# Attention and MoE on one core: an order dropped from ACT's late work, and the power-of-two products moved to the transposes' banks

## The chip, the cores and the metric

The kernel runs on one core of one Trainium2 chip. The metric is the device time of one execution in microseconds. TensorE is called PE here, VectorE DVE, ScalarE ACT, GpSimd POOL, and SP is the queue that issues most transfers.

## The reference

Four batches, eight heads, 576 positions, head size 64. The attention has a bias that a small network computes from positions; its result goes through a gated MoE layer of width 512 and 1536.

```python
scores = scale * np.matmul(q, k.transpose(0, 1, 3, 2))
x = (psi_rel / psi_i)[..., None]
h = np.maximum(x @ w1 + b1, 0.0)
bias = h @ w2
scores = scores + bias.transpose(2, 0, 1)[None, :, :, :]
scores = scores - np.max(scores, axis=-1, keepdims=True)
attn = np.exp(scores)
attn = attn / (np.sum(attn, axis=-1, keepdims=True) + 1e-09)
attn_out = np.matmul(attn, v)
...
a = x @ w_a
b = x @ w_b
return (a * b @ w_out)
```

All inputs and outputs are float32.

## The kernel before, in words

**Tiles.** A unit is a batch, a pair of heads (A and B) and one of two chunks of rows (`UNITS`). Each unit has four tiles of 128 rows by 576 columns, in the second chunk a fifth for the left-over rows. `TILES` lists 144 tiles; the first 16 belong to the first four units (`u < NP`, `N0 = 16`), "opening" tiles here. They take their operands as float32; the later units split values into two 16-bit or rounded parts.

**One tile** goes through `attn_steps` in pieces. `qk_pair` (L450, for opening tiles two at a time) or `qk` (L428) makes the scores on PE. `soft1` (L465) adds the bias and takes the row minimum on DVE (L472), then the exponential on ACT (L477). One step later `soft2` (L500) forms the reciprocal of the row sum (L505 on POOL, L506 on DVE) and scales the row on POOL (L508). Two steps later `turn` (L514) transposes five blocks on PE (L521) into the tile `tp`. For an opening tile ACT copies it to SBUF in one piece (L526). For a later tile ACT casts it to float16 (L538), and DVE forms the rest: L539 for blocks 0 to 3 on all partitions, L540 for block 4, from partitions 64 to 127 only. Then `pv_first` (L480) or `pv` (L547) multiplies with the values into a PSUM tile of tag `pv` and splits the result into two float16 parts (ACT L495 and DVE L496; ACT L567 and DVE L569).

**PSUM.** A bank holds 2 KB per partition, which is 512 float32 numbers. `qk` takes two banks, `tp` (five blocks of 128 columns) takes two, of which the second holds block 4 alone, and `pv` takes one. All of these have one buffer, so `turn` and `pv` wait until the last reader of the former tile is done.

**Powers of two.** The values of a batch (`v_scale`, L189) and each group of four weight chunks (`wab_steps`, L297) are scaled by powers of two. ACT sums magnitudes along rows (L200, L266). `pow2_down` (L62) turns the column of sums into a row with a small product (L64) against the unit matrix, on one partition (values) or four (weights). DVE takes the maximum (L66), bounds it and keeps the exponent (L67, L68) and forms a diagonal (L72). `pow2_up` (L75) spreads the result over the 128 partitions with a second small product (L77), which DVE copies out (L79). Each of the two products, called `pr`, takes a tile of tag `pv` and so shares its one bank with the attention output. There are ten pairs in all. For the weights the second product, and with it the scaling (L283 on POOL, L286 on ACT, L287 on POOL), comes two steps of that generator after the first.

**Weights.** `w_load` (L235) issues the transfer of a chunk on SP, `w_unit` (L241) converts 64-bit bit patterns to float32 on ACT and DVE (L244 to L249).

**What sets the order.** On PE the order is that of the program text (`manual_schedule`). The generators for attention, weights and MoE are interleaved by `merge` in fixed proportions. On the other engines and on SP a planner orders instructions from their dependencies and its own estimate of when each is ready. `issue_after` adds an order between two instructions of one engine, without a wait for the end of the first. `late()` (L172) uses it: work traced inside goes behind the last score reduction on DVE (`ttrs`), the last exponential (`exps`) and the last opening copy on ACT (`evs`), and the last scaling on POOL (`pns`) traced so far. `evs` is filled only by opening tiles. Inside `late()` stand L200, the weight conversion and the parts of the weights, and the preparation of keys, queries and values of later units; the transfers follow `paced()`, behind the last bias transfer on SP.

**After the opening**, MoE blocks (`moe_block`, L635) are merged with the attention of the next batch: 24 products a chunk (L649) into one bank, the first 12 into its first half and the other 12 into its second half; ACT reads the first half (L657), DVE the second (L659).

Of the kernel before, what the change touches and what calls it, by code (L numbers as in the profile page):

```python
# [7 lines left out]
F32 = mybir.dt.float32  # L8
# [39 lines left out]
def attention_moe(ctx, tc, q0d, q1d, kd, vd, idn, wp, wa, wb, wo, lsw, lg, rl, out):  # L48
    nc = tc.nc
# [7 lines left out]
    g_d = dram.tile([FC, 128, TOK], F32, name="g_d")  # L57
    winv = cst.tile([128, FC, 2], F32, name="winv")
    xt, cpool, epool, xpool = [], [None], [None], [None]
    vsc = []  # L60

    def pow2_down(mx, n, tag):  # L62
        ps = pvp.tile([128, 512], F32, tag="pv", name="pr")
        nc.tensor.matmul(ps[0:n, 0:128], mx, tab["idn"], start=True, stop=True)  # L64
        m = att.tile([n, 1], F32, tag="p2m" + tag, name="p2m", bufs=2)
        nc.vector.reduce_max(out=m, in_=ps[0:n, 0:128], axis=AX.X)  # L66
        nc.vector.tensor_scalar(out=m, in0=m, scalar1=3.0e38, scalar2=2.0 ** -100, op0=ALU.min, op1=ALU.max)  # L67
        nc.vector.tensor_scalar(  # L68
            out=m.bitcast(I32), in0=m.bitcast(I32), scalar1=0x7F800000, scalar2=None, op0=ALU.bitwise_and
        )  # L70
        dg = att.tile([n, n], F32, tag="p2d" + tag, name="p2d", bufs=2)
        nc.vector.tensor_scalar(out=dg, in0=tab["idn"][0:n, 0:n], scalar1=m, scalar2=None, op0=ALU.mult)  # L72
        return dg

    def pow2_up(dg, n, tag):  # L75
        ps = pvp.tile([128, 512], F32, tag="pv", name="pr")
        nc.tensor.matmul(ps[:, 0:n], tab["one"][0:n, :], dg, start=True, stop=True)  # L77
        g = att.tile([128, n], F32, tag="p2g" + tag, name="p2g", bufs=2)
        nc.vector.tensor_copy(g, ps[:, 0:n])  # L79
        return g  # L80
# [85 lines left out]
        return tc.issue_after(rows_in[-1].ins) if rows_in else nullcontext()  # L166


    ttrs, exps, evs, pns = [], [], [], []

    @contextmanager
    def late():  # L172
        with ExitStack() as s:
            for x in (ttrs, exps, evs, pns):
                if x:
                    s.enter_context(tc.issue_after(x[-1].ins))
            yield
# [11 lines left out]
    def v_scale(b):  # L189
        mx = att.tile([128, NP], F32, tag="vmx", name="vmx", bufs=2)  # L190
        vfs = [load_v(b, hp) for hp in range(2)] if b else []
        yield
        for hp in range(NP):
            if b:
                junk = vf = vfs[hp]
            else:
                vf = st["vs", hp].rearrange("p x j d -> p (x j d)")
                junk = att.tile([128, 640], F32, tag="rv", name="junk", bufs=2)
            with late():
                nc.scalar.activation(junk, vf, AF.Abs, accum_out=mx[:, hp:hp + 1])  # L200
            junk = vf = None
            if b:
                vfs[hp] = None
                if hp + 2 < NP:
                    vfs.append(load_v(b, hp + 2))
            yield
        m1 = att.tile([128, 1], F32, tag="vm1", name="vm1", bufs=2)
        nc.vector.reduce_max(out=m1, in_=mx, axis=AX.X)
        dg = pow2_down(m1, 1, "v")
        yield  # L210
        if b:
            yield
        vsc.append(v_scales(pow2_up(dg, 1, "v"), b))
        yield
# [42 lines left out]
    def wab_conv(wt, raw):  # L257
        with late():
            return w_unit(wt, raw)

    def wab_size(f, j, wf, m):
        nm = "ab"[j]
        w16[nm, f] = w16t[:, f, j]
        c = 2 * (f % 2) + j
        with late():
            nc.scalar.activation(  # L266
                w16[nm, f][:, 0], wf.rearrange("p (k n) -> p k n", k=KC), AF.Abs, accum_out=m[:, c:c + 1]
            )
# [28 lines left out]
    def wab_steps(wt):  # L297
# [10 lines left out]
        for s in range(4 * np_ + 7):  # L308
            p, c = divmod(s - 7, 4)
            if 0 <= p < np_:  # L310
                if c == 0:
                    rms[p] = wab_scale(p, pow2_up(dgs.pop(p), 4, "w"))
                with late():
                    wab_parts(p, c, wfs.pop(s - 7), rms[p])
            p, c = divmod(s - 5, 4)
            if 0 <= p < np_ and c == 0:
                dgs[p] = pow2_down(ms.pop(p), 4, "w")
            if 1 <= s <= 4 * np_:
                p, c = divmod(s - 1, 4)
                if c == 0:  # L320
                    ms[p] = att.tile([128, 4], F32, tag="wm", name="wm", bufs=2)
                wab_size(2 * p + c // 2, c % 2, wfs[s - 1], ms[p])
            if s < 4 * np_:
                wfs[s] = wab_conv(*raws.pop(s))
                if s % 4 == 1 and s // 4 + 1 < np_:
                    fetch(s // 4 + 1)
            yield
# [14 lines left out]
    st = {}  # L342
# [171 lines left out]
    def turn(n, pool):  # L514
        u, t = TILES[n]
        c = UNITS[u][2]
        p = st.pop(("pn", n))
        tp = pool.tile([128, 5, 128], F32, tag="tp", name="tp", bufs=1)
        for x in range(5):
            c0 = min(128 * x, S - 128)  # L520
            nc.tensor.transpose(tp[:, x, :], p[:, c0:c0 + 128], tab["idn"])  # L521
        if u < NP:
            if t[0] == "A":
                st["pt", u] = epool[0].tile([128, 5, 256], F32, tag="pt", name="ptf", bufs=2)
            o = 128 * (t[0] == "B")
            evs.append(nc.scalar.copy(st["pt", u][:, :, o:o + 128], tp))  # L526
            return
        W = 512 + 128 * c
        if t in ("A0", "A2"):
            st["pt", u] = cpool[0].tile([128, 9, W], F16, tag="pt", name="pt", bufs=2)  # L530
        pt = st["pt", u]
        if t == "T":
            dst = pt.rearrange("p x (h w) -> p x h w", h=2)[:, :, :, 0:64]
            src = tp.rearrange("p x (h w) -> p x h w", h=2)
        else:
            o = {"A0": 0, "A1": 128, "B0": 256, "B1": 384, "A2": 64, "A3": 192, "B2": 384, "B3": 512}[t]
            dst, src = pt[:, :, o:o + 128], tp
        nc.scalar.copy(dst[:, 0:5], src)  # L538
        nc.vector.tensor_tensor(out=dst[:, 5:9], in0=src[:, 0:4], in1=dst[:, 0:4], op=ALU.subtract)  # L539
        nc.vector.tensor_tensor(  # L540
            out=dst[0:64, 4], in0=src[64:128, 4], in1=dst[64:128, 4], op=ALU.subtract
        )
# [33 lines left out]
    def attn_steps():  # L576
        vgen = [None]
        for n in range(NT + 3):
# [42 lines left out]
            if n >= 2 and n - 2 < NT:  # L621
                turn(n - 2, tpp)
# [120 lines left out]
    chunk_pool(0)  # L743
    qkp = ctx.enter_context(tc.tile_pool(name="qk0", bufs=1, space=PSUM))
    tpp = ctx.enter_context(tc.tile_pool(name="tp0", bufs=1, space=PSUM))
    pvp = ctx.enter_context(tc.tile_pool(name="pv0", bufs=1, space=PSUM))
    ctx.enter_context(tc.manual_schedule(engines={mybir.EngineType.PE}))
    wstack = ctx.enter_context(ExitStack())
# [140 lines left out]
```

## Time and profile before

| what | value |
|---|---|
| three runs, median (lowest to highest) | 876.42 us (870.93 to 877.58) |
| the profiled execution | 875.48 us |
| its span, first to last instruction | 873.4 us |
| mean granted clock of the PE | 0.945 |
| busy of the span | PE 780.3 us, DVE 546.0, ACT 512.5, POOL 308.4 |

The span is cut into stretches in the rows below. A line of the timeline is one instruction, or several in a row: start, duration, engine, line, operation, what it writes and reads, and in brackets how long the engine sat idle before it and what ended that. A line of the waits sums such idle times by who waited for whom. The granted clock is a share of 2.4 GHz; 0.50 is the lower of the two levels.

### The profile page before, as it was taken

To read this page: it belongs to the slowest core of one execution; us is meant where nothing else is said; L and a number is where in the kernel's file an instruction comes from. 1 tells how busy PE (TensorE), PEld (TensorE's weight loads), DVE (VectorE), ACT (ScalarE), POOL (GpSimd) and SP (SyncE) were. 2 spreads that over 40 slices of the span, in tenths; PEclk is the share of its full clock that TensorE was granted. 3 is DMA by queue.
4 is the path that set the end of the run, shared out by engine and by line. 5 is a ranking of instruction groups with operands and counts; after the bars stand their busy time and mean duration, and the time that the engine had idled before them with its cause. 6 is when DMAs were issued, how large, how long until landed. Compare 5 with 4: busy or idle time off the path is not lost.

```text
span 873.4 us, 16482 instructions
## 1 busy us (share of the span) xinstructions
PE 780.3 (89%) x5936; PEld 622.9 (71%) x5936; DVE 546.0 (63%) x1291; ACT 512.5 (59%) x1102; POOL 308.4 (35%) x480
## 2 busy tenths in 40 slices
PE   5865669878888698988999999999999999999998
PEld 1244446647777466765888888888898898888886
DVE  5545577879799667765587778777787665210100
ACT  4747557857686467764577667766776666331310
POOL 0022446747366412321244433432443344220210
PEclk9959688969998799999999999999999999999999
DMA  7897265724776345443444444444443432100001
GB/s 214 242 298 237 77 217 185 208 60 126 232 231 186 91 141 163 139 120 100 127 126 130 130 139 147 118 133 137 117 121 125 127 87 65 55 2 25 1 10 39
DMA packets 52596, 114.16 MB, mean 131 GB/s; under 512 B 5156, under 2 KB 9508, under 8 KB 52516
## 3 DMA queue, kind: packets, MB, share of 16 engines
q1 hardware_dynamic: 44336, 97.34, 36.9%
q10 hardware_dynamic: 8180, 15.77, 6.1%
q8 instruction: 47, 0.77, 0.4%
q14 instruction: 33, 0.27, 0.1%
HBM read 95.91 MB, written 17.18 MB: 129 GB/s over the span
## 4 chain that ended last, share of the span: by engine, by line
PE 66%; DVE 11%; DMA 10%; ACT 6%; issue 4%; SPq 1%; POOL 1%; ACTq 0%; DVEq 0%; POOLq 0%
PE ab L649 25%; PE o L698 17%; PE tp L521 8%; PE qk L444 8%; PE pv L555 5%; PE psta L136 3%; DMA rv<-vd 2%; DMA wraw<-wb 2%; DVE p L472 2%; DMA bias<-bias_d 2%; ACT p L477 1%; DVE ks L373 1%; DVE wt L246 1%; DVE wt L249 1%; DMA rvf<-vd 1%
## 5 line engine op out<-in xcount | busy, mean ns | idle before, releaser
L649 PEld LDWEIGHTS <-w16t 128*128 128x128 f16 x2592 | 254.1, 99 | 44.2 <-issue 12.7
L649 PE MATMUL ab<-x,w16t 128*128 128x256 f16 x2304 | 276.5, 277 | 0.0
L472 DVE CUSTOM_DVE_ANT_0 p<-qk,bias 128x576 f32<-128x576 f32 x144 | 108.7, 755 | 90.4 <-PE tp L521 80.1
L508 POOL TENSOR_SCALAR p<-p,rc 128x576 f32<-128x576 f32 x144 | 126.5, 879 | 70.9 <-DVE rc L506 64.2
L538 ACT CAST pt<-tp 128x640 f16<-128x640 f32 x128 | 88.3, 690 | 101.9 <-PE tp L521 101.4
L477 ACT ACTIVATE p<-p,mn 128x576 f32<-128x576 f32 x144 | 111.7, 776 | 47.6 <-DVE mn L472 45.3
L521 PE MATMUL tp<-idn,p 128*128 128x128 f32 x720 | 111.7, 289 | 20.3 <-DVE pt L540 8.1
L505 POOL TENSOR_SCALAR rr<-sm 128x1 f32<-128x1 f32 x144 | 31.2, 217 | 278.0 <-ACT p L477 274.8
L698 PE MATMUL o<-wos,gh 128*128 128x512 f32 x384 | 124.4, 405 | 0.0
L674 POOL TENSOR_TENSOR gl<-g,gh 128x256 fp32r<-128x256 f32 x96 | 72.6, 758 | 132.0 <-ACT gh L673 130.8
L521 PEld LDWEIGHTS tp<-idn,p 128*128 128x128 f32 x720 | 87.8, 148 | 39.0 <-issue 19.9
L539 DVE TENSOR_TENSOR pt<-tp,pt 128x512 f16<-128x512 f32 x128 | 88.0, 688 | 8.6 <-ACT pt L538 8.3
L659 DVE SCALAR_TENSOR_TENSOR g<-ab,wv,asb 128x256 f32<-128x256 f32 x84 | 40.3, 482 | 82.2 <-ACT asb L657 80.9
L698 PEld LDWEIGHTS o<-wos,gh 128*128 128x128 f32 x384 | 69.1, 190 | 17.8 <-issue 5.4
L444 PE MATMUL qk<-ks,qs 128*128 128x288 f32 x384 | 73.2, 313 | 4.9 <-DVE mn L472 3.8
L698 PE MATMUL o<-wos,gl 128*128 128x512 f32 x192 | 75.8, 395 | 0.0
L136 PE MATMUL psta<-h,w2s 128*32 128x288 f32 (+17 forms) x352 | 48.7, 558 | 25.4 <-ACT bo L154 12.2
L444 PEld LDWEIGHTS qk<-ks,qs 128*128 128x128 f32 x384 | 57.3, 192 | 10.5 <-DVE mn L472 5.3
L657 ACT ACTIVATE asb<-ab,wv 128x256 f32<-128x256 f32 x84 | 39.2, 468 | 40.4 <-PE ab L649 40.3
L673 ACT CAST gh<-g 128x256 fp32r<-128x256 f32 x96 | 38.7, 405 | 35.1 <-DVE g L659 34.8
L555 PE MATMUL pv<-pt,vs 128*64 128x320 f16 (+1 forms) x784 | 56.5, 298 | 0.0
L126 DVE TENSOR_SCALAR h<-u,lgs 128x576 f32<-128x576 f32 (+17 forms) x117 | 46.4, 456 | 14.9 <-PE psta L136 14.5
(92 smaller groups left out, 977.0 us busy)
## 6 DMA issues: line engine op xcount, KB each, us to landing
bias<-bias_d SPq DMA_DIRECT2D x128, 288.0 KB
rv<-vd SPq DMA_DIRECT2D x40, 320.0 KB
bias_d<-bo ACTq DMA_DIRECT2D x36, 295.5 KB
rk<-kd SPq DMA_DIRECT2D x24, 288.0 KB
wraw<-wa SPq DMA_DIRECT2D x12, 512.0 KB
wraw<-wb SPq DMA_DIRECT2D x12, 512.0 KB
wraw<-wo SPq DMA_DIRECT2D x12, 512.0 KB
rq<-q1d SPq DMA_DIRECT2D x16, 320.0 KB
```

What stands on the lines that cost most here:

```text
L136: nc.tensor.matmul(dst[32 * g:32 * g + 32], tab["w2"], hs[g][:, c0:c1], start=True, stop=True)
L444: nc.tensor.matmul(ps[:, hf, :HB], a, b[:, hf * HB:hf * HB + HB], start=(x == 0), stop=(x == len(prods) - 1))
L472: ttr = nc.vector.tensor_tensor_reduce(out=p.rearrange("p (a n) -> p a n", a=2), in0=ps[:, :, :HB], in1=bt.rearrange("p (a n) -> p a n", a=2),
L477: exps.append(nc.scalar.activation(p, p, AF.Exp, bias=mn, scale=-1.0, accum_out=sm))
L508: nc.gpsimd.tensor_scalar(out=p, in0=p, scalar1=rc, scalar2=1.0, op0=ALU.mult, op1=ALU.mult)
L521: nc.tensor.transpose(tp[:, x, :], p[:, c0:c0 + 128], tab["idn"])
L538: nc.scalar.copy(dst[:, 0:5], src)
L539: nc.vector.tensor_tensor(out=dst[:, 5:9], in0=src[:, 0:4], in1=dst[:, 0:4], op=ALU.subtract)
L555: nc.tensor.matmul(ps[64 * j:64 * j + 64, :N], vs[:, part, vb, j, :], pt[:, pb, j * N:j * N + N], start=(x == 0), stop=(x == len(TERMS) - 1),)
L649: nc.tensor.matmul(ab[:, j], w16[nm, f][:, pw, kk, :], xs[px][:, kk, :], start=(x % (3 * KC) == 0), stop=(x % (3 * KC) == 3 * KC - 1),)
L674: nc.gpsimd.tensor_tensor(out=gl, in0=g, in1=gh.bitcast(F32), op=ALU.subtract)
L698: nc.tensor.matmul(o, g[:, sl], wos[f][:, p], start=(f == 0 and x == 0), stop=(f == FC - 1 and x == 2))
```

## The change

The list `evs` goes, and with it the order of late ACT work behind the last opening copy. The `tp` tile is no longer allocated for each transpose: one tile of eight blocks of 128 columns (the same two banks) is allocated once, and the transposes write its blocks 0 to 4. A new function `pr_tile` hands out blocks 6 and 7 of it in turn, and both small products write there in place of a tile of tag `pv`.

```diff
--- before.py
+++ after.py
@@ -57,10 +57,17 @@
     g_d = dram.tile([FC, 128, TOK], F32, name="g_d")
     winv = cst.tile([128, FC, 2], F32, name="winv")
     xt, cpool, epool, xpool = [], [None], [None], [None]
-    vsc = []
+    vsc, tpt = [], []
+
+    prs = [0]
+
+    def pr_tile():
+        prs[0] ^= 1
+        return tpt[0][:, 6 + prs[0], :]
+
 
     def pow2_down(mx, n, tag):
-        ps = pvp.tile([128, 512], F32, tag="pv", name="pr")
+        ps = pr_tile()
         nc.tensor.matmul(ps[0:n, 0:128], mx, tab["idn"], start=True, stop=True)
         m = att.tile([n, 1], F32, tag="p2m" + tag, name="p2m", bufs=2)
         nc.vector.reduce_max(out=m, in_=ps[0:n, 0:128], axis=AX.X)
@@ -73,7 +80,7 @@
         return dg
 
     def pow2_up(dg, n, tag):
-        ps = pvp.tile([128, 512], F32, tag="pv", name="pr")
+        ps = pr_tile()
         nc.tensor.matmul(ps[:, 0:n], tab["one"][0:n, :], dg, start=True, stop=True)
         g = att.tile([128, n], F32, tag="p2g" + tag, name="p2g", bufs=2)
         nc.vector.tensor_copy(g, ps[:, 0:n])
@@ -166,12 +173,12 @@
         return tc.issue_after(rows_in[-1].ins) if rows_in else nullcontext()
 
 
-    ttrs, exps, evs, pns = [], [], [], []
+    ttrs, exps, pns = [], [], []
 
     @contextmanager
     def late():
         with ExitStack() as s:
-            for x in (ttrs, exps, evs, pns):
+            for x in (ttrs, exps, pns):
                 if x:
                     s.enter_context(tc.issue_after(x[-1].ins))
             yield
@@ -515,7 +522,7 @@
         u, t = TILES[n]
         c = UNITS[u][2]
         p = st.pop(("pn", n))
-        tp = pool.tile([128, 5, 128], F32, tag="tp", name="tp", bufs=1)
+        tp = tpt[0][:, 0:5, :]
         for x in range(5):
             c0 = min(128 * x, S - 128)
             nc.tensor.transpose(tp[:, x, :], p[:, c0:c0 + 128], tab["idn"])
@@ -523,7 +530,7 @@
             if t[0] == "A":
                 st["pt", u] = epool[0].tile([128, 5, 256], F32, tag="pt", name="ptf", bufs=2)
             o = 128 * (t[0] == "B")
-            evs.append(nc.scalar.copy(st["pt", u][:, :, o:o + 128], tp))
+            nc.scalar.copy(st["pt", u][:, :, o:o + 128], tp)
             return
         W = 512 + 128 * c
         if t in ("A0", "A2"):
@@ -743,6 +750,7 @@
     chunk_pool(0)
     qkp = ctx.enter_context(tc.tile_pool(name="qk0", bufs=1, space=PSUM))
     tpp = ctx.enter_context(tc.tile_pool(name="tp0", bufs=1, space=PSUM))
+    tpt.append(tpp.tile([128, 8, 128], F32, name="tp"))
     pvp = ctx.enter_context(tc.tile_pool(name="pv0", bufs=1, space=PSUM))
     ctx.enter_context(tc.manual_schedule(engines={mybir.EngineType.PE}))
     wstack = ctx.enter_context(ExitStack())
```

## Rows read from the trace of the kernel before

**Rows 1.** Stretches (us): busy PE, PEld, DVE, ACT, POOL; granted clock, DMA share, GB/s

```profile
46.00:125.00 79.00, 52.63 (x323) 36.29 (x323) 43.34 (x124) 46.95 (x108) 28.01 (x48) 0.73 0.62 203
125.00:180.00 55.00, 39.59 (x272) 28.82 (x272) 46.73 (x107) 40.99 (x93) 36.21 (x43) 0.88 0.65 193
180.00:300.00 120.00, 100.58 (x791) 80.77 (x790) 102.00 (x230) 79.15 (x163) 67.86 (x80) 0.90 0.53 161
400.00:757.00 357.00, 352.76 (x2865) 305.45 (x2863) 248.40 (x581) 224.64 (x479) 130.47 (x235) 1.00 0.39 116
```

**Rows 2.** Waits from 46 to 300 us: us in total, times, longest

```profile
ACT ptf L526 <- PE tp L521: 12.7, 8, 4.6
PE pr L77 <- DVE x L496: 9.1, 2, 5.6
PE tp L521 <- DVE pt L540: 8.1, 5, 3.0
PE pr L64 <- DVE x L496: 8.0, 3, 4.8
PE pr L64 <- DVE x L569: 5.9, 1, 5.9
ACT rv L200 <- DMA rv<-vd: 4.8, 3, 2.3
```

**Rows 3.** Chain that ended last, closing MoE stage: start us, us

```profile
804.84 31.45 PE ab L649 x288
```

**Rows 4.** Timeline of that stage, ACT: start us, us

```profile
807.52 0.47 ACT L657 ACTIVATE asb<-ab,wv 128x256 f32<-128x256 f32 x1 [2.05 <-PE ab L649]
810.14 0.47 ACT L657 ACTIVATE asb<-ab,wv 128x256 f32<-128x256 f32 x1 [1.12 <-PE ab L649]
```

**Rows 5.** Timeline from 84 to 89 us

```profile
84.89 0.16 DVE L208 TENSOR_REDUCE vm<-vmx 128x1 f32<-128x4 f32 x1 [0.72 <-ACT rv L200]
85.92 0.67 ACT L526 COPY ptf<-tp 128x640 f32<-128x640 f32 x1
88.48 0.58 PE L64 MATMUL pr<-idn,vm 128*1 128x128 f32 x2 [4.76 <-DVE x L496]
```

**Rows 6.** Timeline from 94 to 100 us

```profile
94.77 0.68 ACT L526 COPY ptf<-tp 128x640 f32<-128x640 f32 x1
98.61 0.58 PE L77 MATMUL pr<-p2d,one 1*128 1x1 f32 x2 [3.56 <-DVE x L496]
99.36 0.15 DVE L79 COPY p2g<-pr 128x1 f32<-128x1 f32 x1
```

**Rows 7.** Timeline from 126 to 131 us

```profile
126.42 0.29 DVE L540 TENSOR_TENSOR pt<-tp,pt 64x128 f16<-64x128 f32 x1
130.26 0.58 PE L77 MATMUL pr<-p2d,one 4*128 4x4 f32 x2 [5.57 <-DVE x L496]
```

**Rows 8.** Timeline from 175 to 182 us

```profile
175.33 0.29 DVE L540 TENSOR_TENSOR pt<-tp,pt 64x128 f16<-64x128 f32 x1
179.45 0.59 PE L64 MATMUL pr<-idn,wm 128*4 128x128 f32 x2 [5.89 <-DVE x L569]
181.06 0.27 DVE L66 TENSOR_REDUCE p2m<-pr 4x1 f32<-4x128 f32 x1
```

**Rows 9.** Timeline, two places where the bank is read late

```profile
155.30 0.38 PE L64 MATMUL pr<-idn,wm 128*4 128x128 f32 x2 [0.59 <-ACT w16t L266]
159.85 0.29 DVE L540 TENSOR_TENSOR pt<-tp,pt 64x128 f16<-64x128 f32 x1
162.17 0.76 DVE L472 CUSTOM_DVE_ANT_0 p<-qk,bias 128x576 f32<-128x576 f32 x1
...
199.09 0.38 PE L64 MATMUL pr<-idn,wm 128*4 128x128 f32 x2 [1.11 <-ACT w16t L266]
203.16 0.29 DVE L540 TENSOR_TENSOR pt<-tp,pt 64x128 f16<-64x128 f32 x1
205.26 0.75 DVE L472 CUSTOM_DVE_ANT_0 p<-qk,bias 128x576 f32<-128x576 f32 x1
```

## The prediction

> **What bounds the kernel now.** I read first the table of stretches. From 400 us to 757 us the PE is busy 352.76 of 357 us at the full clock of 2.4 GHz, and the change touches nothing there; what can move lies ahead of it [rows 1]. From 46 to 125 us the PE is busy 52.63 of 79 us at a granted clock of 0.73, with DVE and ACT a little over half busy: a stretch of latencies, in which engines wait for one another in turn. From 125 to 300 us DVE is busy 148.7 of 175 us and comes close to being the bound, while the PE still idles for some 35 us.
>
> Then the waits of this stretch, by who released them [rows 2]. Of the PE's idle time the largest shares stand before the tiny power-of-two products (name pr): 9.1 us in two waits and 8.0 us in three for the second half of the attention output (x, L496), which empties the one bank that pr shares with pv, and 5.9 us for the same step of the later tiles (L569). These 23.0 us are what the second part of the change aims at. 8.1 us are transposes that wait for the last reading of their bank (L540). ACT idles 12.7 us ahead of the eight opening copies (L526) that wait for the transposes.
>
> **What a product waits for in its new place.** Blocks 6 and 7 lie in the second 2 KB of the tile, with block 4, the fifth transpose. Does a write to an unread part of a bank wait for a reader of another part? In the closing MoE stage 288 products run without a gap from 804.84 us for 31.45 us [rows 3], 24 to a chunk, so 2.62 us a chunk. L657 reads only the first half of a chunk's bank, which is written after 1.31 us; it starts at 807.52 and 810.14 us, that is at 804.84 plus 2.62 and 5.24, when the second half is done too [rows 4]. So this program orders work by bank, and I take it that pr will wait until ACT's copy (L526, later L538) and DVE's L540 have read block 4.
>
> The Trainium skill says why (PSUM — Partial Sum Buffer, section "PSUM bank collisions raise a hardware error"): two engines may not be in the same bank on the same 32 partitions at once, at other columns either, so software orders by bank and quarter of the partitions, not by address. On the bank the trace agrees, 2.62 us a chunk and not 1.31; no row here shows the quarter. By the quarter the sum would be 868.0 us in place of 870.5 (third rival, worked out there).
>
> **The change, part by part.**
>
> (a) The products leave pv's bank: 20 uses of two PE passes each, unchanged in number and length. Four long stalls matter; the others are short or bound by their own operand.
> 1. The product at 88.48 us: its operand's reduction ended at 85.05 us, and the copy of block 4 ends at 85.92 + 0.67 = 86.59 us [rows 5]. Gain 1.9 us.
> 2. The product at 98.61 us: the copy ends at 95.45 us, so 3.1 us at most. But the product after it, in the same bank, needs L79, which stands on DVE at 99.36 us behind weight work [rows 6]. If that order stays the gain is 0. The order of DVE is planned anew, so I take half, 1.5 us.
> 3. The product at 130.26 us: L540 ends at 126.42 + 0.29 = 126.71 us [rows 7]; raw 3.5 us. DVE has little slack from here on, so I take 3.0.
> 4. The product at 179.45 us: L540 ended at 175.62 us, raw 3.8 us. The next product waits for L66 at 181.06 us, which is queued on DVE [rows 8]. Bounds 0 and 3.8, taken 1.9.
> Together 8.3 us, between 0 and 12.3.
>
> (b) The same products now wait where they did not before. After 125 us the reading of block 4 ends with L540, deep in a busy DVE queue. In seven places the trace has pr before the L540 of the tile transposed just ahead of it. The two worst: pr at 155.30 us, L540 ending at 160.14; pr at 199.09, L540 ending at 203.45 [rows 9]. The other five are 1.2 to 2.9 us each, and the seven add to 18.3 us of PE time. Behind the waiting product stand MoE products, the next scores, and through them the score reduction L472 on DVE. Only what arrives later than DVE would have taken it costs. At 155.30 some 2.9 us of PE work follow, so the scores would end at about 163.1 us where L472 started at 162.17: 0.9 us. At 199.09 some 4.2 us follow: 207.7 against 205.26, 2.5 us [rows 9]. In the other five DVE would come later anyway. Taken 3.4 us, bounds 0 and 18.3.
>
> (c) The transposes' tile is now allocated once. Blocks 0 to 3, in the first bank, may start after L539; only block 4 waits for L540, of 0.29 us. On the 8.1 us in five waits [rows 2] that is at most some 2 us; DVE is the later one there, so I take 0.7. The cost on this side is that block 4 must also wait for L66 or L79 to have read the product. In the trace these reads end before the fifth transpose of the next tile, or within a few tenths of it: nothing, so long as DVE keeps that order.
>
> (d) Late work on ACT (the sums of magnitudes L200 and L266, the weight conversion L244, the casts L286) need no longer follow the last opening copy. It still follows the last exponential, so it can rise only into the idle time ahead of a copy, and this is only while the first 16 tiles are turned; afterwards the removed order held nothing back. In about three of the eight idles [rows 2] an operation of 0.6 to 0.7 us that needs no new data directly follows the copy, and its rise would start the next exponential up to 1 us sooner. Against that: a fetched tile that is late in truth now holds up the copy behind it. L200 already waits 4.8 us in three waits for its transfer [rows 2], but there the copy stands behind it already. Bounds: 4 us lost, 3 won; taken 1.0 won. The transfers themselves are on SP; earlier reading frees their buffers sooner by the same 1 us at most.
>
> The sum: 8.3 + 0.7 + 1.0 - 3.4 = 6.6 us. Not all will reach the end: later stretches have their own limits (transfers, a busy DVE), so I let three quarters through, 5.0 us. Against the profiled execution of 875.48 us (span 873.4) that is 870.5 us. The median of the three times shown is 876.42, 0.94 us above the profiled one.
>
> **Rivals.**
> - The planner follows. DVE's and ACT's orders are made from the dependencies; with the new ones L66 and L79 rise and L540 is drawn ahead. Then (a) is had in full, 12.3 us, (b) costs nothing: 12.3 + 0.7 + 1.0 = 14.0, or 861.5 us. For it: in rows 6 and 8 the reductions stand behind work that was put there because the product was due late. Against: DVE has little room after 125 us.
> - The stall only moves. Places 2 and 4 gain nothing because the reading on DVE stays where it was; with 1.9 + 3.0 - 3.4 the time is 874.0 us.
> - Order by quarters of a bank. The first product of a pair writes one or four partitions, L540 reads partitions 64 to 127 (L540 in the code). If the order is kept for each 32 partitions, first products wait for ACT's copy alone. Both waits priced in (b) belong to first products (L64), so (b) falls to nothing, and three quarters of 10.0 us gives 868.0 us. Rows 4 can't tell, since both sides there use all partitions.
> - Slower: the bank that the products now share is read later than the one they left. Where DVE keeps L540 as late as in rows 9 and has no slack before the next L472, all seven waits pass through: 18.3 us against the 6.4 us of places 1 to 3, so 875.5 + 11.9 = 887.4 us. It decides from 139 us on. For it: DVE is busy 85% there. Against: in five of the seven places DVE would not have been ready.
>
> **How the numbers follow.** Chances: forecast 0.36, planner follows 0.20, stall moves 0.15, quarters 0.12, slower 0.17. About 1% (8.8 us) is what a measurement of this kernel can tell from no change. Below 867.7 us lie all of "planner follows", half of "quarters" and three tenths of the forecast: 0.37. Above 885.2 us lies most of the last: 0.16. The rest, 0.47, is within 1%. The range reaches from 858, where (a), (c) and (d) are had at their best (12.3 + 2 + 3), to 885 at the slower case's near edge; the forecast's own range is 866 to 876.
>
> **What would show it.** In the changed profile no pr may wait for L496 or L569 any more. If I am right, waits of pr for L526, L538 or L540 stand in their place, about half as long in total before 180 us; the PE's busy share from 46 to 180 us rises and with it the granted clock; L472 starts sooner after the stalls at 130 and 179 us. Wrong in (b) if pr never waits for L540, or if such waits add to 10 us or more with DVE idle behind them. Wrong in (d) if ACT's waits for transfers grow by more than 2 us with an opening copy queued behind them. From 400 us on nothing should differ but the start.

## The result and the profile after

| | before | after |
|---|---|---|
| median of 20 runs each, us | 875.96 (870.93 to 879.60) | 883.88 (876.51 to 889.59) |
| after / before, 95% interval | | 1.009 (1.0069 to 1.0112) |
| span of the profiled execution, us | 873.4 | 886.0 |
| mean granted clock | 0.945 | 0.927 |

The change makes the kernel 7.9 us slower by the medians. 870.5 us was forecast, a gain; the time lies inside the range (858 to 885), near its slow edge, on the wrong side of no change. The two profiled executions differ by 12.6 us, more than the medians, because after's is one of its longer ones, 4 us above the median. The readings below are of these two executions and account for those 12.6 us. After's line numbers are before's plus seven (L64 is L71, L540 is L547), and the product's tile is now named `tp`.

The table of stretches after, which answers to [rows 1] (same columns):

```profile
46.00:125.00 79.00, 55.03 (x305) 37.30 (x303) 44.09 (x124) 46.75 (x107) 27.19 (x48) 0.67 0.63 202
125.00:180.00 55.00, 44.16 (x292) 31.88 (x290) 42.36 (x98) 38.20 (x86) 30.21 (x38) 0.81 0.61 183
180.00:300.00 120.00, 99.22 (x749) 78.86 (x748) 100.52 (x218) 78.56 (x162) 65.65 (x77) 0.86 0.50 156
400.00:757.00 357.00, 350.30 (x2845) 302.00 (x2844) 252.57 (x588) 227.80 (x487) 132.69 (x238) 0.99 0.41 119
```

Read the counts and the clock, not the busy time. From 125 to 180 us the PE is busy for longer than before (44.16 against 39.59 us), with 20 instructions more, at a clock of 0.81 against 0.88: it works more slowly. So the prediction's sign, a busy share from 46 to 180 us that rises and the granted clock with it, came only in its first half, and a higher busy share alone is no gain. From 180 to 300 us 749 instructions run where 791 ran. From 400 us nothing is new: the work comes later and takes as long.

The waits after from 46 to 300 us, by who waited for whom, which answer to [rows 2] (total us, times, longest; rows that bear on the argument):

```profile
PE tp L71 <- ACT ptf L533: 6.0, 4, 2.9
PE tp L528 <- DVE pt L547: 5.9, 4, 3.0
ACT rv L207 <- DMA rv<-vd: 5.1, 4, 2.1
PE tp L71 <- ACT rv L207: 5.0, 1, 5.0
PE tp L84 <- DVE pt L547: 4.7, 2, 2.3
PE tp L71 <- DVE pt L547: 3.9, 2, 2.0
...
PE tp L84 <- ACT wt L251: 2.6, 1, 2.6
...
PE tp L528 <- DVE p2g L86: 2.5, 2, 1.3
...
PE tp L71 <- ACT x L574: 1.7, 1, 1.7
```

No product waits for the attention output any more: the 23.0 us behind L496 and L569 are gone. In their place stand 6.0 us behind the opening copy (L533) and 4.7 + 3.9 us behind the reading of block 4 (L547). Three more rows belong there, though the profile names ACT in them. L207 (5.0 us) sums magnitudes of values, but the product that waits there is one of the weights. The timeline shows the real releaser: L547 ends at 162.11 + 0.29 = 162.40 us, and the product starts 0.15 us later. So it is with the other two: L547 ends at 147.34 and 181.59 us, the products start at 147.49 and 181.74. In all, seven waits of 17.9 us stand behind L547, and with the 6.0 us the 23.0 us have come back whole under other names. One row is new in kind: transposes (L528) wait 2.5 us for the reading of a product (L86). The timeline at the place of 5.0 us, which is the first of [rows 9], and at the second:

```profile
162.11 0.29 DVE L547 TENSOR_TENSOR pt<-tp,pt 64x128 f16<-64x128 f32 x1
162.55 0.58 PE L71 MATMUL tp<-idn,wm 128*4 128x128 f32 x2 [5.00 <-ACT rv L207]
167.83 0.76 DVE L479 CUSTOM_DVE_ANT_0 p<-qk,bias 128x576 f32<-128x576 f32 x1 [1.09 <-PE tp L528]
...
207.16 0.29 DVE L547 TENSOR_TENSOR pt<-tp,pt 64x128 f16<-64x128 f32 x1
207.60 0.59 PE L71 MATMUL tp<-idn,wm 128*4 128x128 f32 x2 [1.91 <-DVE pt L547]
208.12 3.90 PE L656 MATMUL ab<-x,w16t 128*128 128x256 f16 x24
213.91 0.76 DVE L479 CUSTOM_DVE_ANT_0 p<-qk,bias 128x576 f32<-128x576 f32 x1 [2.12 <-PE tp L528]
```

Follow the second place. In [rows 9] the product ran at 199.09 us, ahead of L540; now it starts 0.15 us after that reading has ended. The 24 MoE products behind it take 3.90 us. Before, they took 2.79:

```profile
199.41 2.79 PE L649 MATMUL ab<-x,w16t 128*128 128x256 f16 x24
```

The difference is the clock: after, the granted clock is 0.50, the lower level, from 208 to 210 us; before, it is 1.00 from 199 to 203 us. DVE's next score reduction (L479) then has been idle for 2.12 us when its scores come: 213.91 us against 205.26.

The starts of the products tell where the time came from. "Shift" is after's start less before's, "step" its change from the line above (us). Fourteen of the twenty products are listed; one of the six left out matters below, the product at 165.08 us, which starts at 170.35 us after (shift +5.3).

```
before   after   shift  step   what released it after
 54.63   57.56   +2.9   +2.9   opening copy L533
 81.39   83.14   +1.8   -1.2   opening copy L533
 88.48   88.61   +0.1   -1.6   opening copy L533   (place 1)
 98.61   94.50   -4.1   -4.2   opening copy L533   (place 2)
 99.56   97.81   -1.8   +2.4   L86, reading of the product before
130.26  127.66   -2.6   -0.9   no wait             (place 3)
139.65  139.96   +0.3   +2.9   L547
146.14  147.49   +1.4   +1.0   L547
155.30  162.55   +7.3   +5.9   L547
179.45  181.74   +2.3   -5.0   L547                (place 4)
194.22  199.52   +5.3   +3.0   L547
199.09  207.60   +8.5   +3.2   L547
271.48  281.17   +9.7   +1.2
279.93  292.23  +12.3   +2.6   L547
end             +12.6
```

The opening products do gain: at 130 us after is 2.6 us ahead. Behind 130 us it loses 15.2 us, and of the seven places with L547 all but place 4 add to that.

What one such stretch costs the PE, between the same two products, before (first line) and after (second):

```profile
139.65:207.90 68.25, 54.84 (x385) 39.07 (x384) 58.68 (x139) 47.05 (x107) 40.29 (x48) 0.87 0.49 142
```

```profile
139.96:216.87 76.91, 59.94 (x385) 41.71 (x385) 58.23 (x137) 45.09 (x101) 37.45 (x46) 0.80 0.42 125
```

The stretch grows by 8.7 us. The same 385 PE instructions take 5.1 us more at the lower clock, and the PE idles 3.6 us more. DVE does almost the same work (58.2 against 58.7 us) and idles 18.7 us in place of 9.6: it waits more, too.

### The profile page after: what moved, and what is told of

It reads as the page before. It is cut to its first block, busy times and chain, and to the rows that moved or that the text cites. A ratio compares the mean times of both kernels' runs of the same rounds, so it can differ in the third digit from the quotient of the medians.

```text
span 886.0 us, 16591 instructions
## 1 busy us (share of the span) xinstructions
PE 792.2 (89%) x5936; PEld 628.8 (71%) x5936; DVE 548.5 (62%) x1291; ACT 513.5 (58%) x1102; POOL 306.0 (35%) x480
## 4 chain that ended last, share of the span: by engine, by line
PE 66%; DVE 10%; DMA 9%; ACT 8%; issue 5%; SPq 1%; POOL 0%; ACTq 0%; DVEq 0%
PE ab L656 24%; PE o L705 17%; PE qk L451 8%; PE tp L528 8%; PE pv L562 5%; DMA rv<-vd 3%; PE psta L143 3%; DVE p L479 2%; DMA bias<-bias_d 2%; ACT p L484 2%; DMA wraw<-wo 1%; DVE wt L253 1%; DMA rvf<-vd 1%; DVE wt L256 1%; DVE wt L252 1%
## 5 line engine op out<-in xcount | busy, mean ns | idle before, releaser
L479 DVE CUSTOM_DVE_ANT_0 p<-qk,bias 128x576 f32<-128x576 f32 x144 | 108.7, 755 | 97.1 <-PE tp L528 85.1
L528 PE MATMUL tp<-idn,p 128*128 128x128 f32 x720 | 112.0, 290 | 20.1 <-DVE pt L547 6.4
L528 PEld LDWEIGHTS tp<-idn,p 128*128 128x128 f32 x720 | 87.7, 147 | 39.5 <-issue 23.0
L546 DVE TENSOR_TENSOR pt<-tp,pt 128x512 f16<-128x512 f32 x128 | 88.0, 688 | 8.7 <-ACT pt L545 8.6
```

What stands on the lines that cost most here:

```text
L479: ttr = nc.vector.tensor_tensor_reduce(out=p.rearrange("p (a n) -> p a n", a=2), in0=ps[:, :, :HB], in1=bt.rearrange("p (a n) -> p a n", a=2),
```

## The experiments

The theory after this reading: late reading. The products moved after 125 us inherit the readers of the transposes' tile, chiefly L547. Rival one: the dropped order (`evs`) lets late ACT work delay the opening copies. Rival two: holding one tile for all transposes costs something by itself. All ratios are to the kernel before on the same chip.

**The order alone.** Before, with `evs` left out of `late()` only.

```diff
-            for x in (ttrs, exps, evs, pns):
+            for x in (ttrs, exps, pns):
```

> The kernel before with only the list of opening copies taken out of the late work's order; products and transposes' tile as before. Late reading (the loss comes from later products that wait in the shared bank for L540): nothing or a small gain, ratio 0.997 to 1.002. Dropped order (the loss comes from fetched work that stands in front of an opening copy): 6 to 9 us slower, ratio 1.007 to 1.010, and the delay is there by the 16th score reduction, at about 112 us.

Measured: 874.47 against 875.84 us, 0.9981 (0.9951 to 1.001).

**The products alone.** After, with `evs` put back in `late()`.

> The changed kernel with the order behind the opening copies put back, so that only the products' place and the one kept tile are new. Late reading: as slow as the changed kernel, ratio 1.007 to 1.011, the loss setting in after 139 us. Dropped order: no slower than before, ratio 0.995 to 1.000, since the four stalls before L496 and L569 are gone.

Measured: 883.01 against 875.84 us, 1.0078 (1.0051 to 1.0105). The two together: all of the loss comes with the products, and the order is worth nothing that can be measured.

**Which products.** The first two pairs of the values and of the weights (four in all, "opening" below) run up to 130 us, the other six ("later") after it. Here only the opening ones use the transposes' tile; `w` tells the four kinds of call apart (values or weights, first or second product).

```diff
-    def pr_tile():
+    def pr_tile(w):
+        i = prs[1][w] = prs[1].get(w, -1) + 1
         prs[0] ^= 1
-        return tpt[0][:, 6 + prs[0], :]
+        return tpt[0][:, 6 + prs[0], :] if i < 2 else pvp.tile([128, 512], F32, tag="pv", name="pr")
```

> The changed kernel with the order dropped, but of the ten pairs of products only the first two of the values and the first two of the weights (those of the opening tiles, up to about 131 us) go to the transposes' banks; the later six pairs stay in pv's bank. Late reading: the 2.6 us that the changed kernel was ahead at the 20th score reduction are kept or mostly kept, ratio 0.994 to 0.999, and no product waits for L540 (here L547 less a few lines). Dropped order: slower than before by 6 to 9 us, ratio 1.007 to 1.010.

Measured: 870.65 against 875.84 us, 0.9936 (0.9911 to 0.996). No product waits for L547 in its trace.

And the reverse, the later ones alone (`i >= 2`):

> The counterpart: the first two pairs of each kind stay in pv's bank, the later six go to the transposes' banks, the order is dropped. Late reading: slower by the whole loss after 139 us without the gain ahead of it, 9 to 14 us, ratio 1.010 to 1.016. Dropped order: slower by 6 to 9 us, with the delay there before 112 us.

Measured: 881.21 against 875.84 us, 1.0059 (1.0032 to 1.0087), less than expected. Its waits from 46 to 300 us (rows of products behind a bank's readers; others left out) show both banks at once:

```profile
PE pr L71 <- DVE x L503: 6.4, 2, 5.4
PE tp L84 <- DVE pt L547: 6.2, 4, 2.3
PE pr L84 <- DVE x L503: 5.3, 2, 3.0
PE tp L71 <- DVE pt L547: 4.9, 2, 3.0
PE tp L71 <- ACT wt L251: 4.9, 1, 4.9
PE tp L71 <- ACT vs L414: 2.9, 1, 2.9
```

The opening products wait for the attention output as before, the later ones for L547: eight waits, 18.9 us with the last two rows, whose products also start 0.15 us after an L547 has ended. So the change consists of a gain up to 130 us and a loss after it. The sizes don't add: 0.9936 and 1.0059 would make no change, and after is at 1.009, so the later products cost more beside moved opening ones (1.009 / 0.9936 = 1.0155) than alone.

**The tile by itself.** Before, with one tile allocated for all transposes and the products left in their old bank.

```diff
+    tpt.append(tpp.tile([128, 8, 128], F32, name="tp"))
...
-        tp = pool.tile([128, 5, 128], F32, tag="tp", name="tp", bufs=1)
+        tp = tpt[0][:, 0:5, :]
```

> The kernel before with only the transposes' tile allocated once for all; products stay in pv's bank, the order behind the opening copies stays. The planner gives the same order on every engine, so only the waits of the transposes change. If the part (c) was sized rightly: 0 to 2 us faster, ratio 0.998 to 1.000, and the 8.1 us of transposes that wait for L540 shrink by 1 to 2 us. A rival in which the kept tile itself costs (more waits on the transposes): slower, ratio above 1.003.

Measured: 875.63 against 875.43 us, 1.0001 (0.9982 to 1.002). Its waits, and the timeline at the end of one:

```profile
PE tp L521 <- DVE pt L540: 8.1, 5, 3.0
```

```profile
261.66 0.29 DVE L540 TENSOR_TENSOR pt<-tp,pt 64x128 f16<-64x128 f32 x1
...
262.10 0.45 PE L521 MATMUL tp<-idn,p 128*128 128x128 f32 x1 [2.98 <-DVE pt L540]
```

The transposes wait for L540 exactly as in [rows 2], 8.1 us in five. The first of them writes block 0, in the other bank from block 4, and starts only after block 4 is read (261.95 us). One tile in place of many costs nothing by itself, and it frees nothing.

**By bank or by tile.** After, with the two readings in `turn` exchanged: block 4 (now L546) ahead of blocks 0 to 3 (now L549).

```diff
-        nc.vector.tensor_tensor(out=dst[:, 5:9], in0=src[:, 0:4], in1=dst[:, 0:4], op=ALU.subtract)
...
+        nc.vector.tensor_tensor(out=dst[:, 5:9], in0=src[:, 0:4], in1=dst[:, 0:4], op=ALU.subtract)
```

> The changed kernel with the two readings of a later tile in the other order: block 4 first, then blocks 0 to 3, so that the bank which the products share comes free 0.7 us sooner and the first bank 0.3 us later. Late reading: some seven to ten waits of products shorter by up to 0.7 us each and what follows from them, 3 to 7 us off the changed kernel, ratio to before 1.001 to 1.006. If the loss has another cause (the order, the planner's new order as such): as slow as the changed kernel, 1.007 to 1.011.

Measured: 881.19 against 875.43 us, 1.0073 (1.0052 to 1.0095), which can't be told from after's 1.009. It lies in the range named for another cause, but the exchange did not free the products sooner, as it was meant to, so the time decides nothing. The timeline shows why:

```profile
156.41 0.29 DVE L546 TENSOR_TENSOR pt<-tp,pt 64x128 f16<-64x128 f32 x1
...
156.72 0.69 DVE L549 TENSOR_TENSOR pt<-tp,pt 128x512 f16<-128x512 f32 x1
...
157.56 0.59 PE L71 MATMUL tp<-idn,wm 128*4 128x128 f32 x2 [4.97 <-DVE pt L549]
```

Block 4 has been read by 156.70 us. The product, which writes block 6 or 7 beside it, starts 0.15 us after L549 has read the *other* bank (157.41 us). So do seven more products of this run. Here the program orders a write behind all readers of the tile, whatever bank they read.

**The order again**, now where the products gain: opening_moved with `evs` kept.

> The opening products alone moved, as in the run opening_moved, but with late work still behind the opening copies. If dropping the order is worth nothing: the same as opening_moved, ratio 0.991 to 0.997. If the order helps (products_moved was 10 us ahead at the 20th score reduction, the changed kernel 2.6): faster than opening_moved by 3 to 8 us, ratio 0.985 to 0.990.

Measured: 871.48 against 875.43 us, 0.9948 (0.9924 to 0.9972), beside 0.9936 without: no difference.

**Out of the way of L547.** The opening products stay in the transposes' tile; the later six go into the MoE products' three banks (tag `ab`).

```diff
-        return tpt[0][:, 6 + prs[0], :]
+        return tpt[0][:, 6 + prs[0], :] if i < 2 else mps.tile([128, 512], F32, tag="ab", name="pr", bufs=3)
```

> Opening products in the transposes' banks as in opening_moved; the later six pairs take a turn in the three buffers of the MoE products (tag ab), whose last readers are two chunks back. Late reading: no product waits for L540 or for L569 any more, 3 to 7 us faster than opening_moved, ratio 0.985 to 0.991. If a later wait takes the place (the next MoE chunk waits for the product's reading on DVE): the same as opening_moved, 0.991 to 0.997, with waits of L649 (here L656) for L66 or L79.

Measured: 866.12 against 875.43 us, 0.9883 (0.9864 to 0.9902). The two longest of the products' waits that are left:

```profile
PE tp L71 <- ACT ptf L533: 8.4, 4, 3.6
...
PE pr L84 <- DVE p2d L79: 6.0, 2, 3.8
```

The first row is opening products behind the copy. The second is a product that waits for its own operand.

**A bank of its own.** The opening products get a bank of a pool that is opened beside that of the bias network (`eq`), the later ones stay in `ab`.

```diff
-        return tpt[0][:, 6 + prs[0], :]
+        return opp[0].tile([128, 512], F32, tag="pr", name="pr", bufs=1) if i < 2 else mps.tile([128, 512], F32, tag="ab", name="pr", bufs=3)
```

> Opening products in a bank of their own (the one that is free until the MoE's three banks are allocated), later products in the MoE rotation as in later_in_ab; the order is dropped. If sharing the transposes' tile costs in the opening too (there 8.4 us of first products wait for the opening copies L533): 2 to 5 us faster than later_in_ab, ratio 0.982 to 0.986. If the opening has other limits (the operand of the product, the readings on DVE, transfers): the same as later_in_ab, 0.986 to 0.991.

Measured: 858.77 against 876.12 us, 0.9800 (0.9782 to 0.9818), faster than either expectation: sharing the transposes' tile costs in the opening too.

The same with `evs` kept:

> As own_bank, with late work kept behind the opening copies. If dropping the order is worth nothing, as opening_order_kept against opening_moved showed: within 0.4% of own_bank. If it helps where no product waits for an opening copy: 3 us or more slower than own_bank.

Measured: 857.55 against 876.12 us, 0.9789 (0.9767 to 0.981): 18.6 us below before, and better than both kernels; it can't be told from own_bank. Its longest waits of products, then the first stretch, here (first line) and in own_bank (second):

```profile
PE pr L71 <- ACT w16t L273: 8.5, 4, 4.0
...
PE pr L84 <- DVE p2d L79: 7.4, 2, 5.3
```

```profile
46.00:125.00 79.00, 54.63 (x373) 38.35 (x374) 51.43 (x146) 54.90 (x127) 39.35 (x57) 0.84 0.75 234
46.00:125.00 79.00, 57.88 (x345) 39.86 (x345) 49.80 (x137) 52.74 (x121) 34.61 (x55) 0.72 0.72 235
```

The products now wait mostly for their own operands (the sums of L273, the diagonal of L79). From 46 to 125 us the PE does 373 instructions where it did 323 in [rows 1], at a clock of 0.84 against 0.73. In own_bank it does 345, at 0.72: more work gets done in both, and the higher clock is not what both share.

**The later products alone in `ab`**, the opening ones in pv's bank as before.

> Opening products in pv's bank as before, only the later six pairs in the MoE rotation; the order is dropped. The share of the gain that comes after 139 us alone: if the waits for L569 and L496 there (5.9 and 5.6 us with the slow clock behind them) are what counts, 4 to 8 us faster than before, ratio 0.991 to 0.995; if most of later_in_ab's gain comes from the opening, 0.996 to 1.000.

Measured: 874.01 against 876.12 us, 0.9964 (0.9938 to 0.999), at the near edge of the range for "mostly the opening"; its interval takes in both ranges.

All ratios with the order dropped, by place:

| | later in `pv` | later in `tp` | later in `ab` |
|---|---|---|---|
| opening in `pv` | 0.9981 | 1.0059 | 0.9964 |
| opening in `tp` | 0.9936 | 1.0090 | 0.9883 |
| opening in own bank | | | 0.9800 |

## Why the prediction was wrong

**The step that failed is (b).** It named the wait, its reason and the two worst places, and then took 3.4 of the raw 18.3 us: "Only what arrives later than DVE would have taken it costs", and "In the other five DVE would come later anyway". Far more passed through. After, seven waits behind L547 add to 17.9 us; six are places that the prediction had listed, and the seventh is place 4, which it had not. At those six the shift grows by 2.9, 1.0, 5.9, 3.0, 3.2 and 2.6 us, 18.6 in all, of which 2.0 are given back at 170.35 us. At 155.30 us a cost of 0.9 us was forecast and L479 came 5.7 us late; at 199.09 us 2.5 were forecast and it came 8.7 us late in all, after a shift of 2.9 us at 190 us. The medians give 18 us as well where the opening products are in `tp`: the later ones in `tp` against `ab` are 1.009 / 0.9883 = 1.021. With the opening ones in `pv` the same step is 1.0059 / 0.9964 = 1.0095, only 8 us of 18.9 us of waits. So (b) was 8 to 18 us, not 3.4, and not always the whole wait.

The working held DVE's times fixed and asked when the PE would come. DVE's reading frees the tile, the product waits for it, the scores stand behind the product, and DVE waits for the scores: one loop, in which a delay on either side can delay both; in the stretch above PE and DVE both idle more. "DVE would come later anyway" was read from a trace without the new waits. Beside that, the work behind the stall ran at a lower clock, 5.1 of the 8.7 us of that stretch, for which the sum had no term.

The loop is not all of it. At the first place of [rows 9] the score reduction just ahead of the one at 167.83 us already came 4.6 us late, and DVE had not been idle before it. Its scores were done by 156.85 us, but the planner had put weight work (L252 to L256) ahead of it. Before, and then after:

```profile
155.52 0.74 DVE L472 CUSTOM_DVE_ANT_0 p<-qk,bias 128x576 f32<-128x576 f32 x1
```

```profile
155.62 1.23 PE L451 MATMUL qk<-rkf,rqf 64*128 64x288 f32 x4
156.79 1.38 DVE L252 TENSOR_SCALAR wt<-wt 128x512 int32<-128x512 int32 x1
...
160.14 0.75 DVE L479 CUSTOM_DVE_ANT_0 p<-qk,bias 128x576 f32<-128x576 f32 x1
```

And from the 21st score reduction to the 52nd after takes 13.5 us longer than before (131.75 to 336.14 us against 134.36 to 325.23), but opening_moved, which keeps the stall of place 4 and has no product waiting for L547, still takes 2.7 us longer than before (132.99 to 326.59). The other 10.8 us go with the place of the later products.

**The premise of (b), order by bank, held for the waits and was still too fine.** The exchanged readings show order by tile. [Rows 4] could not tell the two apart, as each product tile there is one bank. The Trainium skill (PSUM — Partial Sum Buffer, section "PSUM bank collisions raise a hardware error") would need order by bank and quarter alone. First products (L71, four partitions) waited at 139.96, 162.55, 181.74 and 207.60 us for L547, which reads partitions 64 to 127: this program's order is coarser than that need. So the rival "quarters" fell.

**(a) was right in size.** The steps at the four places are 1.6, 4.2, 0.9 and 5.0 us, 11.7 against the 8.3 taken and 12.3 at most. Of this, 2.4 us of place 2 are lost at the very next product, which waits for the reading of the one before, as the prediction and its rival "the stall only moves" had feared; and 2.0 of place 4 had been given back before it. Some 7.3 us remain, so the size was right and the split over places was off. Opening_moved shows the first three places alone: 0.9936. But a wait was missed in it: the product at 54.63 us, which waited for nothing in before, now stands behind an opening copy, and that copy behind a weight chunk whose transfer is late:

```profile
56.26 0.66 ACT L251 ACTIVATE wt<-wraw 128x512 f32<-128x512 f32 x1 [2.97 <-DMA wraw<-wa]
56.83 0.68 ACT L533 COPY ptf<-tp 128x640 f32<-128x640 f32 x1
57.56 0.58 PE L71 MATMUL tp<-idn,vm 128*1 128x128 f32 x2 [2.94 <-ACT ptf L533]
...
62.05 1.30 PE L528 MATMUL tp<-idn,p 128*128 128x128 f32 x5 [1.16 <-DVE p2g L86]
```

It cost 2.9 us there, of which 0.6 were left at the next product (60.31 us against 59.72). The last line belongs to (c).

**(c) fell on both sides.** Blocks 0 to 3 can't start after L539: 0.7 us was taken, and tile_kept gave 1.0001 with the 8.1 us unchanged. The cost that was put at "nothing", transposes that wait for L66 or L79 to have read the product, was there: 2.5 us in two waits for L86, 1.2 of them at 62.05 us, where the shift grows from 0.6 to 1.8 us.

**(d) came to nothing.** 1.0 us was taken. Kept or dropped, the order made no measurable difference in four pairs (1 and 0.9981, 1.0078 and 1.009, 0.9948 and 0.9936, 0.9789 and 0.98). The sign against it did not come either: ACT's waits for the transfer of values went from 4.8 to 5.1 us.

**The rival "slower" is what happened**, from 139 us on, though it had all waits pass. Its sum gave 887.4 us; the profiled execution, 12.6 us of span above before's 875.48, lies at 888.0, the median at 883.9. That it met the 888.0 is in part luck: to 130 us after gained 2.6 us, not 6.4, and behind it lost 15.2, not 18.3. The argument held against it, that in five places DVE would not have been ready, was the failed step again. "Planner follows" had L540 drawn ahead; at both places of [rows 9] L547 comes later than L540 had (162.11 and 207.16 us). The test named for (b), waits behind L540 of 10 us or more with DVE idle behind them, was met with 17.9 us.

**What stays open.** Later products in `tp` cost 0.8% where the opening ones are in `pv` (1.0059 / 0.9981) and 1.55% where they are in `tp` (1.009 / 0.9936), and the gains of `ab` don't add to those of the opening either (0.9964, 0.9936, together 0.9883). One explanation is that the planner makes another order for each kernel, as at 160.14 us above; no run held DVE's order, so its share in the loss is not known. Single profiled executions also scatter: the span of order_dropped is 5.4 us below before's, its median 1.4 us.

## What to carry to other kernels

A small product placed in a "free" part of a tile that something else uses inherits every reader of that tile, other banks included; before moving it, list those readers and where each stands in its engine's queue, and look first for a bank that nobody reads late (0.979 here against 1.009). When a new wait closes a loop between two engines, don't hold one engine's times fixed and take the wait at next to nothing: let the range reach up to the whole wait (here 8 of 18.9 us in one pair of runs, 18 of 17.9 in another), and add what the work behind it loses at a lower clock.

## What the runs showed of the hardware

With five new stalls of 1.7 to 5.0 us in 77 us, the PE's own work got longer: the same 385 instructions took 54.84 us at a granted clock of 0.87 and 59.94 us at 0.80, and one run of 24 MoE products 3.90 us, most of it at 0.50, in place of 2.79 at 1.00. In this stretch that was more than the added idle time (5.1 against 3.6 us).
